# On-chip tiles declared in another order in a two-block attention decode kernel: the ring buffers start at byte 20480 of a partition instead of 16512

## The chip, the cores and the metric

The kernel runs on one core of a Trainium2 chip. The core has five engines that run side by side, each with its own instruction stream: TensorE (PE in the profile, with PEld for the loads of its weights), VectorE (DVE), ScalarE (ACT), GpSimd (POOL) and SyncE (SP). Data lies in the chip's main memory (DRAM in the program's names), in an on-chip tile memory of 128 partitions, and in a smaller accumulator memory that matmuls write. Sixteen DMA engines move data between main memory and the tile memory; SP and ACT issue transfers to them through queues of their own (q1 and q10 in the profile). Engines wait for each other and for transfers through semaphores.

The metric is the device time of one execution in microseconds. Before the change it is 1944.66 us, the median of 3 runs (1944.61 to 1944.73).

## What is computed

Two independent attention blocks, A and B, of the same shape: 2 batch rows, one query position, 32 heads of 192 elements, and a key and a value cache of 8192 positions for each head, all in bf16. The results stand side by side in the output of 2 x 1 x 1280.

```python
q = (x @ wq).reshape(B, Sq, H, Dh).transpose(0, 2, 1, 3)
scores = jnp.einsum("bhqd,bhkd->bhqk", q, k_cache) * (Dh ** -0.5)
p = softmax(scores, axis=-1)
o = jnp.einsum("bhqk,bhkd->bhqd", p, v_cache)
return o.transpose(0, 2, 1, 3).reshape(B, Sq, H * Dh) @ wo
# reference: concatenate([block(A), block(B)], axis=-1)
```

Each element of the caches is read once and used once. The caches of a block are 2 x 2 x 32 x 8192 x 192 x 2 B, so together they are 805 MB of the 836.77 MB that the profile counts as read.

## The kernel before

**Pairs.** The work is cut into 64 pairs of heads (2 blocks x 2 batch rows x 16). The K cache of a pair is 6,291,456 contiguous bytes. `kv_src` lays them over the 128 partitions, 49,152 B for each, so that partitions 0 to 63 hold the first head and 64 to 127 the second, with 128 positions in each partition. The V cache of a pair is laid out the same way.

**Tiles and their addresses.** `sb` allocates a tile of the tile memory. Tiles stand one behind the other in the order in which they are declared, each with the same address in every partition, and the first one of the kernel stands at byte 16512. In the order of the declarations these are three ring buffers (`ring`, 49,152 B in each partition), two product tiles (`prod`, 12,288 B), the q row (`qrow`, 12,288 B), then `qt`, `sc`, `pb` and a long list of small tiles, of which `filler` (1024 B) is one of the last. The two tiles of the result, `out_sb`, come almost at the end.

**Loads.** SP issues every large load, in the order of `order`: the q weights of both blocks first (each in two parts, one into a ring buffer, one into a product tile), then K and V of pair 0, K and V of pair 1, and so on; the last four are K, K, V, V. `next_slot` hands out the three ring buffers in turn. Before it reuses a buffer, SP waits until its last reader is done (`free`): the fourth multiply of a pair for K, the last matmul of the weighted sum for V. Behind the caches come the output weights `wo` in eleven pieces (`WA`, `WB`), which go into ring buffers as these come free; they are 160 to 3040 KB. The two loads of x and half of the stores of the result go through ACT's queue.

**One pair.** `add_q` copies the q of a pair into all partitions by a matmul, and `add_qt` takes it to the tile memory (`qt`). In four quarters VectorE multiplies K by q into `prod` (`add_mul`, line 290), TensorE sums over the 192 elements with twelve matmuls against the identity (`add_sum`, line 295), and VectorE reduces the 16 sums that are left into `sc` (`add_red`, line 301). Maximum (VectorE, GpSimd), exponential (ScalarE, into `pb`, line 322) and 64 matmuls of V with `pb` (line 334) follow. `add_fill` puts twelve matmuls on `filler` between them, whose results nobody reads. `add_place` collects the results of the heads, and at the end `add_contract` multiplies them by `wo`, ScalarE takes the sums to `out_sb`, and four small stores write the output.

**Loop.** VectorE, ScalarE and TensorE run pairs 2 to 61 in a hardware loop of three pairs a pass (`LOOP`), so a buffer with number i % 3 has a fixed address within a pass. SP's stream is written out.

The parts of the code that the change and the prediction speak of:

```python
ring = [sb(f"ring{i}", [128, RW], BF16) for i in range(3)]
prod = [sb(f"prod{i}", [128, TQ * Dh], BF16) for i in range(2)]
qrow = sb("qrow", [34, N], BF16)
...
load((kind, i), s, ring[s][:], src, free[s])
...
S_dve.add(lambda eng, t: eng.tensor_tensor(pr3(qd), quarter(i, qd), q, ALU.mult), waits=w, sig=("m", i, qd))
```

Of the kernel before, what the change touches and what calls it, by code (L numbers as in the profile page):

```python
# [8 lines left out]
BF16 = mybir.dt.bfloat16  # L9
F32 = mybir.dt.float32  # L10
# [91 lines left out]
def build_kernel(nc, blocks, out):  # L102
    NBLK = len(blocks)
    B, Hn, Sk, Dh = blocks[0]["k"].shape
# [6 lines left out]
    T = 128  # L111
    NB = 3
# [22 lines left out]
    with ExitStack() as es:  # L135
        sb = lambda name, shape, dt: es.enter_context(nc.sbuf_tensor(name, shape, dt))
        ps = lambda name, shape, dt: es.enter_context(nc.psum_tensor(name, shape, dt))
        sem = lambda name: es.enter_context(nc.semaphore(name))

        ring = [sb(f"ring{i}", [128, RW], BF16) for i in range(3)]  # L140
        prod = [sb(f"prod{i}", [128, TQ * Dh], BF16) for i in range(2)]
        qrow = sb("qrow", [34, N], BF16)
        qt = [sb(f"qt{i}", [128, Dh], BF16) for i in range(3)]
        sc = [sb(f"sc{i}", [128, T], F32) for i in range(NB)]
        pb = [sb(f"pb{i}", [128, T // 2, 34], BF16) for i in range(NB)]
        mp = [sb(f"mp{i}", [128, 2], F32) for i in range(NB)]
        mg = [sb(f"mg{i}", [128, 2], F32) for i in range(NB)]
# [8 lines left out]
        sel = sb("sel", [34, NBLK * B, 128], BF16)  # L156
        place = sb("place", [2, 264], BF16)
        ones = sb("ones", [128, 1], F32)
        filler = sb("filler", [128, 512], BF16)
        oallS = [sb(f"oallS{k}", [128, WR, 2], BF16) for k in range(NBLK)]  # L160
        out_sb = [sb(f"out_sb{k}", [34, NH2], BF16) for k in range(NBLK)]
        actd = sb("actd", [128, 2], F32)
# [360 lines left out]
def bass_concat_heads__gqa_block_cached__mha_block_cached__decode_kernel(  # L523
    nc: bass.Bass,
    A_x: bass.AP,
    A_k_cache: bass.AP,
    A_v_cache: bass.AP,
    A_wq: bass.AP,
    A_wo: bass.AP,
    B_x: bass.AP,  # L530
    B_k_cache: bass.AP,
    B_v_cache: bass.AP,
    B_wq: bass.AP,
    B_wo: bass.AP,
    out: bass.AP,
):
    blocks = [
        dict(x=A_x, k=A_k_cache, v=A_v_cache, wq=A_wq, wo=A_wo),
        dict(x=B_x, k=B_k_cache, v=B_v_cache, wq=B_wq, wo=B_wo),
    ]  # L540
    build_kernel(nc, blocks, out)
# [28 lines left out]
```

## Time and profile before

| What | Value |
|---|---|
| Median of 3 runs | 1944.66 us (1944.61 to 1944.73) |
| Execution that was profiled | 1944.61 us |
| Its span, first to last instruction | 1942.8 us |
| Mean granted TensorE clock | 0.996 |
| Read from main memory | 836.77 MB, 431 GB/s over the span |
| ACT busy | 187.0 us (10%) |
| POOL busy | 35.1 us (2%) |

The profile is one execution, recorded by the hardware. Its span leaves out what lies before the first and behind the last instruction of the program, 1.8 us here. Rows of the groups of instructions give line, engine, operation, what is written and read, and the count, then the total busy time and the mean time of one, then the idle time of the engine just before them and what ended most of it. A row of the waits names who waited for whom, with the total, the number of times and the longest. A DMA row gives the packets, the megabytes and the time that the packets took, as a share of the time of all 16 DMA engines in the stretch; a packet belongs to the stretch in which it starts. In the list of transfers the last number is the median time from issue to landing. The chain of waits is followed back from the last instruction to what released each step; its rows here are start, length and what it was, and "issue" is time in which the engine waited for nothing that the profile shows.

### The profile page before, as it was taken

To read this page: it belongs to the slowest core of one execution; us is meant where nothing else is said; L and a number is where in the kernel's file an instruction comes from. 1 tells how busy PE (TensorE), PEld (TensorE's weight loads), DVE (VectorE), ACT (ScalarE), POOL (GpSimd) and SP (SyncE) were. 2 spreads that over 40 slices of the span, in tenths; PEclk is the share of its full clock that TensorE was granted. 3 is DMA by queue.
4 is the path that set the end of the run, shared out by engine and by line. 5 is a ranking of instruction groups with operands and counts; after the bars stand their busy time and mean duration, and the time that the engine had idled before them with its cause. 6 is when DMAs were issued, how large, how long until landed. Compare 5 with 4: busy or idle time off the path is not lost.

```text
span 1942.8 us, 21605 instructions
## 1 busy us (share of the span) xinstructions
PE 1643.4 (85%) x8715; PEld 787.7 (41%) x8715; DVE 1081.4 (56%) x834; ACT 187.0 (10%) x608; POOL 35.1 (2%) x88
## 2 busy tenths in 40 slices
PE   4888888888888888888888888888888888888888
PEld 1343443443443443443443443443443443443434
DVE  0556546556646646656646646655645645655660
ACT  2111011011011011011011001001001001001000
POOL 1000000000000000000000000000000000000000
PEclk9999999999999999999999999999999999999999
DMA  9999999999999999999999999999999999999998
GB/s 414 430 431 434 434 431 432 435 434 430 432 436 433 428 435 434 432 430 436 434 429 432 437 433 429 433 436 434 429 433 434 434 430 434 433 433 431 435 427 377
DMA packets 20774, 836.98 MB, mean 431 GB/s; under 512 B 2316, under 2 KB 2584, under 8 KB 2968
## 3 DMA queue, kind: packets, MB, share of 16 engines
q1 hardware_dynamic: 20744, 836.78, 99.8%
q8 instruction: 10, 0.16, 0.0%
q14 instruction: 4, 0.03, 0.0%
q10 hardware_dynamic: 16, 0.01, 0.0%
HBM read 836.77 MB, written 0.01 MB: 431 GB/s over the span
## 4 chain that ended last, share of the span: by engine, by line
issue 87%; PE 4%; DMA 4%; DVE 3%; POOL 1%; ACT 0%; SPq 0%; POOLq 0%; DVEq 0%; ACTq 0%
DVE prod L290 2%; PE ops L334 2%; DMA ring<-in_B_wq_dram 2%; DMA ring<-in_B_k_cache_dram 1%; POOL mg L310 1%; PE scps L295 1%; DMA ring<-in_B_wo_dram 1%; PE ops L259 1%; DVE sc L301 0%; PE outps L342 0%; ACT pb L322 0%; PE outps L392 0%; SPq L189 0%; POOLq L49 0%; DVE mp L307 0%
## 5 line engine op out<-in xcount | busy, mean ns | idle before, releaser
L290 DVE TENSOR_TENSOR prod<-ring,qt 128x6144 bf16<-128x6144 bf16 x256 | 852.8, 3352 | 694.3 <-DMA ring<-in_B_k_cache_dram 324.3
L295 PE MATMUL scps<-prod,ident 128*128 128x512 bf16 x3072 | 709.1, 381 | 208.5 <-DVE prod L290 208.5
L334 PE MATMUL ops<-ring,pb 128*34 128x384 bf16 x4096 | 676.8, 326 | 0.0
L295 PEld LDWEIGHTS scps<-prod,ident 128*128 128x128 bf16 x3072 | 280.4, 98 | 614.6 <-DVE prod L290 309.0
L334 PEld LDWEIGHTS ops<-ring,pb 128*34 128x34 bf16 x4096 | 395.5, 98 | 258.7
L301 DVE TENSOR_REDUCE sc<-scps 128x32 f32<-128x512 f32 x256 | 175.6, 686 | 109.7 <-PE scps L295 109.7
L342 PE MATMUL outps<-filler,ident 128*128 128x512 bf16 x768 | 176.9, 380 | 0.0
L342 PEld LDWEIGHTS outps<-filler,ident 128*128 128x128 bf16 x768 | 70.1, 98 | 78.3
L357 ACT ACTIVATE oodd<-ops 2x192 f32<-2x192 f32 x64 | 20.6, 322 | 690.3 <-PE ops L334 690.3
L283 ACT ACTIVATE qt<-qps 64x192 bf16<-64x192 f32 x64 | 20.7, 324 | 662.5 <-PE qps L277 662.5
L322 ACT ACTIVATE pb<-sc,nb 64x128 bf16<-64x128 f32 x128 | 81.5, 637 | 7.8
L347 PE MATMUL ops<-ones,rs 128*2 128x1 f32 x128 | 12.2, 164 | 56.7 <-ACT pb L322 56.7
L310 POOL PARTITION_ALL_REDUCE mg<-mp x64 | 26.0, 406 | 1850.7 <-DVE mp L307 1850.7
L315 ACT ACTIVATE nb<-mg 64x1 f32<-64x1 f32 x64 | 13.0, 203 | 331.1 <-POOL mg L310 331.1
L347 PEld LDWEIGHTS ops<-ones,rs 128*2 128x2 f32 x128 | 5.5, 82 | 87.8 <-ACT pb L322 87.3
L322 ACT ACTIVATION_READ_ACCUMULATOR pb<-sc,nb 64x1 f32 x128 | 38.4, 300 | 0.0
L259 PE MATMUL ops<-ring,xT 128*2 128x512 bf16 x96 | 28.1, 420 | 6.2 <-issue 4.1
L277 PE MATMUL qps<-qrow,sel 34*128 (+1 forms) x64 | 21.3, 333 | 1.4 <-ACT qt L284 0.8
L377 PEld LDWEIGHTS oall<-on,place 2*128 (+1 forms) x256 | 10.3, 92 | 29.3 <-issue 26.3
L306 DVE TENSOR_REDUCE mp<-sc 64x1 f32<-64x128 f32 x64 | 17.8, 278 | 7.6
L361 DVE RECIPROCAL rc<-ops 2x1 f32<-2x1 f32 x64 | 9.4, 146 | 21.2 <-PE ops L334 21.2
L363 DVE TENSOR_TENSOR oodd<-ops,oodd 2x192 f32<-2x192 f32 x64 | 20.9, 326 | 0.4 <-ACT oodd L357 0.4
(43 smaller groups left out, 172.4 us busy)
## 6 DMA issues: line engine op xcount, KB each, us to landing
ring<-in_A_k_cache_dram SPq DMA_DIRECT2D x32, 6144.0 KB, 26.4
ring<-in_A_v_cache_dram SPq DMA_DIRECT2D x32, 6144.0 KB, 29.2
ring<-in_B_k_cache_dram SPq DMA_DIRECT2D x32, 6144.0 KB, 26.4
ring<-in_B_v_cache_dram SPq DMA_DIRECT2D x31, 6144.0 KB, 29.2
ring<-in_A_wq_dram SPq DMA_DIRECT2D x1, 6144.0 KB, 17.6
ring<-in_B_wq_dram SPq DMA_DIRECT2D x1, 6144.0 KB, 35.4
ring<-in_B_v_cache_dram SPq DMA_DIRECT2D x2, 3072.0 KB, 25.4
ring<-in_A_wo_dram SPq DMA_DIRECT2D x2, 3040.0 KB, 21.4
```

The lines of the kernel that those rows point to most:

```text
L259: ins = eng.matmul(ops[n % 2][32 * blk:32 * blk + 2, 0:QC], xT[:, c, 2 * blk:2 * blk + 2], src, start=(c == 0), stop=(c == DC - 1))
L277: return eng.matmul(qps[:, 0:2 * Dh], sel[:].rearrange("p s m -> p (s m)")[:, bass.ds(k, 128)], qrow[:, bass.ds(c, 2 * Dh)], start=True, s ...
L283: eng.activation(qt[i % 3][0:64, :], qps[0:64, 0:Dh], ACTF.Identity)
L290: S_dve.add(lambda eng, t: eng.tensor_tensor(pr3(qd), quarter(i, qd), q, ALU.mult), waits=w, sig=("m", i, qd))
L295: ins = eng.matmul(scps[qd % 2][:], ident[:], pr3(qd)[:, :, j * DG:(j + 1) * DG], start=(j == 0), stop=(j == NJ - 1))
L301: S_dve.add(lambda eng, t: eng.tensor_reduce(sc[i % NB][:, qd * TQ:(qd + 1) * TQ], scps[qd % 2][:], AXL.X, ALU.add), waits=[("s", i, qd), ...
L310: S_pool.add(lambda eng, t: eng.partition_all_reduce(mg[i % NB][:], mp[i % NB][:], 128, bass.bass_isa.ReduceOp.max), waits=[("mx", i), key ...
L322: ins = eng.activation(pb[i % NB][p0:p0 + 64, :, h::32], sc[i % NB][p0:p0 + 64, :].rearrange("p (j a) -> p j a", a=2), ACTF.Exp, bias=nb[i ...
L334: ins = eng.matmul(ops[i % NB][0:34, 0:2 * Dh], pb[i % NB][:, j, :], vv[:, j, :], start=(j == 0), stop=(j == T // 2 - 1))
L342: ins = eng.matmul(to, ident[:], filler[:], start=True, stop=True)
L357: S_act.add(lambda eng, t: eng.activation(oodd[i % NB][:], ops[i % NB][32:34, Dh:2 * Dh], ACTF.Identity), waits=[("pv", i), key("on", i - ...
L363: S_dve.add(lambda eng, t: eng.tensor_tensor(oodd[i % NB][:], ops[i % NB][0:2, 0:Dh], oodd[i % NB][:], ALU.add), waits=[("od", i)], sig=(" ...
```

## The change

The declarations of `qt`, `sc` and `filler` move in front of the ring buffers, and a tile `spare` of 256 B in each partition, which nothing reads or writes, is put between them. Everything else in the program is the same.

```diff
+        qt = [sb(f"qt{i}", [128, Dh], BF16) for i in range(3)]
+        sc = [sb(f"sc{i}", [128, T], F32) for i in range(NB)]
+        filler = sb("filler", [128, 512], BF16)
+        sb("spare", [128, 64], F32)
         ring = [sb(f"ring{i}", [128, RW], BF16) for i in range(3)]
         prod = [sb(f"prod{i}", [128, TQ * Dh], BF16) for i in range(2)]
         qrow = sb("qrow", [34, N], BF16)
-        qt = [sb(f"qt{i}", [128, Dh], BF16) for i in range(3)]
-        sc = [sb(f"sc{i}", [128, T], F32) for i in range(NB)]
         pb = [sb(f"pb{i}", [128, T // 2, 34], BF16) for i in range(NB)]
...
         ones = sb("ones", [128, 1], F32)
-        filler = sb("filler", [128, 512], BF16)
         oallS = [sb(f"oallS{k}", [128, WR, 2], BF16) for k in range(NBLK)]
```

## The prediction

> **What bounds the kernel now.** I read the page first: engine shares, DMA row, queue shares, transfer times.
>
> ```profile
> span 1942.8 us, 21605 instructions
> PE 1643.4 (85%) x8715; PEld 787.7 (41%) x8715; DVE 1081.4 (56%) x834; ACT 187.0 (10%) x608; POOL 35.1 (2%) x88
> ...
> DMA packets 20774, 836.98 MB, mean 431 GB/s; under 512 B 2316, under 2 KB 2584, under 8 KB 2968
> ...
> q1 hardware_dynamic: 20744, 836.78, 99.8%
> ...
> ring<-in_A_k_cache_dram SPq DMA_DIRECT2D x32, 6144.0 KB, 26.4
> ring<-in_A_v_cache_dram SPq DMA_DIRECT2D x32, 6144.0 KB, 29.2
> ```
>
> Queue q1, SP's loads, keeps the 16 DMA engines busy 99.8% of the span; no compute engine is above 85%. A K load lands 26.4 us after its issue and a V load 29.2 us. Then the waits of the engines, with those of SP's queue:
>
> ```profile
> DVE prod L290 <- DMA ring<-in_B_k_cache_dram: 324.3, 31, 10.7
> DVE prod L290 <- DMA ring<-in_A_k_cache_dram: 316.0, 31, 10.7
> ...
> SPq L189 <- PE ops L334: 1078.7, 64, 17.0
> SPq L189 <- DVE prod L290: 738.4, 64, 17.8
> ```
>
> VectorE waits for the K load of nearly every pair, about 10.3 us each time (640.3 / 62). SP waits as well, for ring buffers to come free, but that costs nothing as long as a transfer is queued ahead. To see this I took the chain of waits for the length of a pair of heads (one K and one V load) and a stretch of 1744.32 us from the middle:
>
> ```profile
> 162.66 28.64 issue
> ...
> 1790.70 28.47 issue
> ```
>
> ```profile
> DMA packets 17286, 754.98 MB, mean 433 GB/s; under 512 B 1920, under 2 KB 1920, under 8 KB 1920
> ...
> q1 hardware_dynamic: 17278, 754.88, 100.2%
> ```
>
> The two chain rows are 56 pairs apart: 1628.04 / 56 = 29.07 us a pair, 14.54 us a load. So a K load has 26.4 - 14.5 = 11.9 us of other transfers ahead of it when issued, a V load 14.7 us. The engines never lack work (100.2% of the stretch, which is over 100 because packets overlap a little). The kernel runs at the pace of its DMA engines, and only what changes their time per byte or per packet moves its end by much.
>
> **What a packet is.** In the stretch 1920 packets are under 512 B: 16 completion words for each of 120 loads. The other 15,358 carry 754.88 MB, 49,152 B each: one packet is one whole row of a ring buffer in one partition. Its start address is the tile's own.
>
> **The change, part by part.** No instruction, wait, transfer or order of issue is added, removed or moved; `spare` has no instruction. What moves is addresses. By the declared sizes, qt takes 3 x 384 B, sc 3 x 512 B, filler 1024 B, spare 256 B: 3968 B, and 16512 + 3968 = 20480, so the change does what it says. Each ring buffer is 49152 B = 12 x 4096, each product tile 12288 B = 3 x 4096: before, every one starts 128 B past a multiple of 4096, after, on one. The tiles from pb to ones move by 1280 B, those behind the filler by 256 B; qt and sc move in front. Their readers and writers are the compute engines, and two small loads and four small stores that lie at the ends.
>
> First, compute. What would it cost if the multiply, the sum matmuls or any small instruction ran differently at the new addresses? Nothing up to the cover: VectorE has about 10.3 us of waiting in each 29.07 us pair, TensorE 15% of the span, 4.4 us a pair. The groups that touch the moved tiles:
>
> ```profile
> L290 DVE TENSOR_TENSOR prod<-ring,qt 128x6144 bf16<-128x6144 bf16 x256 | 852.8, 3352 | 694.3 <-DMA ring<-in_B_k_cache_dram 324.3
> L295 PE MATMUL scps<-prod,ident 128*128 128x512 bf16 x3072 | 709.1, 381 | 208.5 <-DVE prod L290 208.5
> L334 PE MATMUL ops<-ring,pb 128*34 128x384 bf16 x4096 | 676.8, 326 | 0.0
> ```
>
> All four multiplies of a pair could become 20% slower (4 x 0.67 = 2.7 us) and the transfers would still be ahead. Without that cover, each 1% of the multiplies would cost 0.134 us a pair, 8.6 us in all. I cost compute at 0, both ways.
>
> Second, the transfers: time per byte and time per packet. The end of the kernel has many loads with short rows, so two stretches separate the two. From 1930 to 1936 us:
>
> ```profile
> DMA packets 430, 2.48 MB, mean 413 GB/s; under 512 B 50, under 2 KB 78, under 8 KB 383
> ...
> q1 hardware_dynamic: 426, 2.48, 99.9%
> ```
>
> Long rows: 100.2% of 1744.32 us x 16 engines, less 1920 words of 9 ns (below), over 15,358 rows = 1819.7 ns for 49,152 B. Short rows: 99.9% of 6 us x 16, less 50 words, over 376 rows = 253.9 ns for 6,596 B on average. The difference, 1565.8 ns for 42,556 B, is 36.79 ps per byte (435 GB/s over 16 engines). What is left, 253.9 - 242.7 = 11 ns, comes with each packet whatever its length; the rounding of the megabytes makes that uncertain by about 0.5 ns. So no part of the present address grows visibly with length: a penalty on every piece of a row is excluded up to the pace of 435 GB/s, and what the change can win lies in those 11 ns. In the stream a row takes 1744.32 / (15,358 / 16) = 1817.2 ns; less 1808.4 for its bytes and 1.1 for an eighth of a word, 7.7 ns. The rest overlaps.
>
> What of it hangs on the address? The rows that differ in little else are the four stores of the result, 640 B each, read from out_sb. With each tile's address rounded up to 32 B, out_sb0 lies at 225,120 and out_sb1 at 225,760, which is 96 and 224 B past a multiple of 256. The first block's two from ScalarE's queue, in 0.1 us; the second block's two from the same queue, then two from SP's, in 0.04 us each; and, in 0.1 us, ScalarE's last two with one completion word:
>
> ```profile
> q10 hardware_dynamic: 2, 0.00, 4.1%
> ```
>
> ```profile
> q10 hardware_dynamic: 2, 0.00, 10.9%
> ```
>
> ```profile
> q1 hardware_dynamic: 2, 0.00, 11.6%
> ```
>
> ```profile
> q10 hardware_dynamic: 3, 0.00, 4.9%
> ```
>
> Shares are of 16 engines: 4.1% x 1600 ns / 2 = 32.8 ns a packet for the first block; 10.9% x 640 / 2 = 34.9 and 11.6% x 640 / 2 = 37.1, mean 36.0, for the second. The same bytes from another phase took 3.2 ns longer. This is a read of the tile memory, where the ring loads write, and few packets. The last row says something else: 78.4 - 69.8 = 9 ns for a completion word, so a packet costs about 9 ns even with next to no data, which speaks for a fixed cost that no address removes.
>
> So a row's gain lies between 0 (all is packet handling) and 7.7 ns (all is the phase); a loss is bounded by the same 7.7 ns, since nothing in the trace shows an address on a multiple of 4096. I take 4.7 ns, a third of the way from the stores' 3.2 to the 7.7, because the stores alone isolate the address. There are 20,744 - 2,316 = 18,428 rows, 1,152 for each engine: 1,152 x 4.7 ns = 5.4 us; the ends are 0 and 8.9 us.
>
> [...]
>
> Third, the ends. Head and tail keep their length: the last piece of wo still lands after everything else, and the last products and the store follow it. The sum: span 1942.8 - 5.4 = 1937.4 us. Around the span lie 1944.61 - 1942.8 = 1.8 us of the profiled execution, which is within 0.05 us of the median of the runs, 1944.66. So 1939.2 us.
>
> **The rivals.** *The cost is the packet's, not the address's.* For it: the completion word's 9 ns with 4 B, near the 11 ns of a row. Against: the stores' 3.2 ns. Time 1944.6 us; a gain under 3.4 ns a row (3.9 us) falls here too.
>
> *All of the 7.7 ns goes.* For it: the long and short rows show one constant and no other term, and all rows share one phase. Against: the word's 9 ns. 1944.6 - 8.9 = 1935.7 us.
>
> *Slower: transfers and engines meet.* On multiples of 4096 the front of each row that is loaded, of the ring buffer that VectorE reads and of the product tile that TensorE reads all share low address bits zero, and if the tile memory serves them in blocks of such addresses, a write waits once a row for an engine's read. With the size that the phase has above, 4.7 ns, each row takes 1821.9 ns: 1944.6 + 5.4 = 1950.0 us. It decides from 3.4 ns a row on. Against: the ring buffers already lie at equal offsets from each other before, with VectorE and TensorE at work, and the stream is within 0.5% of its pace per byte. [...]
>
> **How the numbers follow.** About 0.2% (3.9 us) is what a measurement of this kernel can tell from no change. Forecast, 1937 to 1940.7 us around 1939.2: 0.53. All of the cost gone, 1934.5 to 1937: 0.09. No visible effect, 1940.8 to 1945: 0.24. Slower, 1948.5 to 1951.5: 0.14. Faster: 0.53 + 0.09 = 0.62; same 0.24; slower 0.14. The range runs from 1936.0 to 1945.2 us; it leaves out the slower case and half of the largest gain, 0.19.
>
> **What would show it.** Right: a pair takes 29.00 us instead of 29.07 in the chain, the middle stretch moves at 434 GB/s, the two-stretch sum leaves 6 to 7 ns a packet instead of 11, and the multiply and the matmuls keep 3352, 381 and 326 ns with VectorE still waiting for K loads. Wrong: the same 29.07 us and 11 ns (the packet's own cost), or a pair above 29.07 us with q1 still at 100% (transfers slowed), or VectorE no longer waiting for K loads (compute slowed beyond its cover).

## The result, and the profile after

The changed kernel takes 1939.87 us, the median of 11 runs (1939.65 to 1940.10), against 1944.61 us before (11 runs, 1944.36 to 1944.86). The ratio is 0.9976 with a 95% interval of 0.9966 to 0.9985: 4.74 us faster. The profiled execution after has a span of 1937.8 us, 5.0 us less. From its page, the engines, the DMA row and the queue:

```profile
span 1937.8 us, 21540 instructions
...
PE 1633.1 (84%) x8650; PEld 787.8 (41%) x8715; DVE 1081.4 (56%) x834; ACT 186.8 (10%) x608; POOL 34.9 (2%) x88
...
DMA packets 20774, 836.98 MB, mean 432 GB/s; under 512 B 2316, under 2 KB 2584, under 8 KB 2968
...
q1 hardware_dynamic: 20744, 836.78, 99.8%
```

Packets, bytes and the share of the load queue are what they were; the same work passes in less time. (The records of 64 matmuls on the filler and of one more matmul are missing from this trace, hence fewer instructions.) The groups that touch the moved tiles, with the wait of the multiply for its K loads:

```profile
L291 DVE TENSOR_TENSOR prod<-ring,qt 128x6144 bf16<-128x6144 bf16 x256 | 852.5, 3351 | 688.9 <-DMA ring<-in_B_k_cache_dram 322.1
L296 PE MATMUL scps<-prod,ident 128*128 128x512 bf16 x3072 | 709.0, 381 | 204.4 <-DVE prod L291 204.4
L335 PE MATMUL ops<-ring,pb 128*34 128x384 bf16 x4096 | 676.8, 326 | 0.0
```

These three kept their durations (3352, 381 and 326 ns before), and VectorE still waits for nearly every K load. The chain of waits, first and last row of the same 56 pairs:

```profile
162.88 28.52 issue
...
1786.88 28.41 issue
```

(1786.88 - 162.88) / 56 = 29.00 us a pair, where it was 29.07. The 56 pairs take 4.04 us less (1628.04 - 1624.00), which for 64 pairs is 4.6 us: the gain is spread over the whole stream of loads and lies in no single place. The DMA rows of the stretch of long rows (100 to 1839.36 us), then of the short rows near the end (1925 to 1931 us):

```profile
DMA packets 17281, 754.79 MB, mean 434 GB/s; under 512 B 1919, under 2 KB 1919, under 8 KB 1919
...
q1 hardware_dynamic: 17273, 754.69, 100.2%
```

```profile
DMA packets 384, 2.54 MB, mean 423 GB/s; under 512 B 43, under 2 KB 45, under 8 KB 311
...
q1 hardware_dynamic: 380, 2.54, 100.7%
```

By the working of the prediction: (100.2% x 1739.36 us x 16 - 1919 x 9 ns) / 15,354 = 1815.0 ns for a long row, 4.7 ns less than before; (100.7% x 6 us x 16 - 43 x 9 ns) / 337 = 285.7 ns for 7,537 B. That is 36.75 ps per byte, as before, and 8.7 ns for each packet, where it was 11.

### The profile page after: what moved, and what is told of

It is laid out like the page before. It is cut to its first block, busy times and chain, and to the rows that moved or that the text cites. A ratio compares the mean times of both kernels' runs of the same rounds, so it can differ in the third digit from the quotient of the medians.

```text
span 1937.8 us, 21540 instructions
## 1 busy us (share of the span) xinstructions
PE 1633.1 (84%) x8650; PEld 787.8 (41%) x8715; DVE 1081.4 (56%) x834; ACT 186.8 (10%) x608; POOL 34.9 (2%) x88
## 3 DMA queue, kind: packets, MB, share of 16 engines
q1 hardware_dynamic: 20744, 836.78, 99.8%
## 4 chain that ended last, share of the span: by engine, by line
issue 87%; PE 4%; DMA 4%; DVE 3%; POOL 1%; ACT 0%; SPq 0%; POOLq 0%; DVEq 0%; ACTq 0%
DVE prod L291 2%; PE ops L335 2%; DMA ring<-in_B_wq_dram 2%; DMA ring<-in_B_k_cache_dram 1%; POOL mg L311 1%; PE scps L296 1%; DMA ring<-in_B_wo_dram 1%; PE ops L260 1%; DVE sc L302 0%; PE outps L343 0%; ACT pb L323 0%; PE outps L393 0%; SPq L190 0%; POOLq L49 0%; DVE mp L308 0%
## 5 line engine op out<-in xcount | busy, mean ns | idle before, releaser
L291 DVE TENSOR_TENSOR prod<-ring,qt 128x6144 bf16<-128x6144 bf16 x256 | 852.5, 3351 | 688.9 <-DMA ring<-in_B_k_cache_dram 322.1
L343 PE MATMUL outps<-filler,ident 128*128 128x512 bf16 x704 | 162.4, 379 | 10.0 <-issue 9.9
```

The costliest lines, as they stand in the source:

```text
L343: ins = eng.matmul(to, ident[:], filler[:], start=True, stop=True)
```

## The experiments

### Which address matters

Four kernels follow, beside 31 runs of the kernel before with a median of 1944.62 us. The first takes the spare tile out of the changed kernel.

```diff
-        sb("spare", [128, 64], F32)
```

> The changed kernel without the spare tile: the ring buffers start at 20224 = 79 x 256, no multiple of 512 or 4096. Theory A (a row that starts 128 B past a multiple of 256 costs some 4 ns, and any multiple of 256 cures it): 1939.9 us. Theory B (the multiple of 4096 matters): 1944.6 us. Theory C (it is the place of qt, sc and filler in front of the ring buffers): 1939.9 us. Theory D (the product tiles' address matters to the engines, not the ring's to the transfers): 1939.9 us, as they move along.

1939.88 us, ratio 0.9975 (0.9966 to 0.9985). B is out: a multiple of 256 does as well as one of 4096. The second leaves the old order and puts 128 B in front.

```diff
+        sb("spare", [128, 32], F32)
         ring = [sb(f"ring{i}", [128, RW], BF16) for i in range(3)]
```

> The kernel before with nothing but a spare tile of 128 B in front of the ring buffers: they start at 16640 = 65 x 256, with qt, sc and filler where they stood, 128 B further. A and D: 1939.9 us. B and C: 1944.6 us.

1939.90 us, ratio 0.9975 (0.9966 to 0.9985). C is out, and one spare tile of 128 B does the whole work of the change. The third keeps the new order and goes off the boundary again.

```diff
-        sb("spare", [128, 64], F32)
+        sb("spare", [128, 96], F32)
```

> The changed kernel with a spare tile of 384 B instead of 256: the new order stays, but the ring buffers start at 20608, again 128 B past a multiple of 256. A, B and D: 1944.6 us. C: 1939.9 us.

1944.44 us, ratio 1.0000 (0.9991 to 1.0009): the gain is gone. The fourth separates the product tiles from the ring.

```diff
+        sb("spare2", [128, 32], F32)
         prod = [sb(f"prod{i}", [128, TQ * Dh], BF16) for i in range(2)]
```

> The changed kernel with 128 B between the ring buffers and the product tiles: the ring stays at 20480, the product tiles and the q row start 128 B past a multiple of 256. A, B and C: 1939.9 us, with all packets of a row still at one duration. D: 1944.6 us.

1939.93 us, ratio 0.9976 (0.9967 to 0.9985). D is out. What counts is the address of the ring buffers, where the loads write, and there only whether a row starts on a multiple of 256 B (16640, 20224 and 20480 do; 16512 and 20608 do not). The source of each row of a ring buffer starts on a multiple of 256 B from the start of its tensor in all these kernels. Whether the boundary counts by itself, or only against the phase of the source, was not tried.

### How far off, and which engine

Four kernels beside 33 runs of before with a median of 1944.24 us. The first two change the spare tile to 320 and 288 B.

```diff
-        sb("spare", [128, 64], F32)
+        sb("spare", [128, 80], F32)
```

> The changed kernel with 320 B spare: the ring buffers start at 20544, 64 B past a multiple of 256. A1 (any start off a multiple of 256 makes one piece more of each row, whatever the distance): 1944.6 us. A2 (cost in proportion to the distance, 4.1 ns a row at 128 B): half of it, 1942.2 us. A3 (a multiple of 64 is enough, 128 is a special case): 1939.9 us.

1944.18 us, ratio 1.0000 (0.9991 to 1.0009).

```diff
-        sb("spare", [128, 64], F32)
+        sb("spare", [128, 72], F32)
```

> The changed kernel with 288 B spare: the ring buffers start at 20512, 32 B past a multiple of 256. A1: 1944.6 us. A2: a quarter, 1941.1 us. A3 (64 is enough): 1944.6 us or more.

1945.45 us, ratio 1.0006 (0.9997 to 1.0015); its lowest run, 1945.18, is above the highest of the runs of before beside it, 1945.05. The traces agree: by their packets a long row takes 1820.8 ns on average from 100 us on with 32 B, and 1819.6 ns in the kernel before. A1's times hold to about 1 us: 64 B off costs what 128 B cost, and 32 B off does not cost a quarter but slightly more than 128. The one piece more of each row that A1 names is a supposition that no run shows. A2 and A3 are out.

The prediction priced the row as if its address cost by itself. Does it take an engine that uses the tile memory at the same time? Two cuts to the kernel before leave out most of what an engine does there. The first multiplies 16 of the 192 elements of each position:

```diff
-        q = qt[i % 3][:].unsqueeze(1).broadcast_to([128, TQ, Dh])
+        q = qt[i % 3][:].unsqueeze(1).broadcast_to([128, TQ, Dh])[:, :, 0:DG]
...
-        eng.tensor_tensor(pr3(qd), quarter(i, qd), q, ALU.mult)
+        eng.tensor_tensor(pr3(qd)[:, :, 0:DG], quarter(i, qd)[:, :, 0:DG], q, ALU.mult)
```

> The kernel before (ring at 16512) with the multiplies cut to 16 of the 192 elements of each position; the scores are sums over what the product tiles held. Theory E1 (the row's extra time comes only while VectorE reads the ring and writes the products): 1939.9 us, long rows at 1815 ns. E2 (while TensorE reads): 1944.6 us. E3 (the address costs by itself, no engine needed): 1944.6 us.

1944.55 us, ratio 1.0001 (0.9991 to 1.0011), with VectorE busy for 347.4 us instead of 1081.4. The second leaves out most of the matmuls:

```diff
-                for j in range(NJ):
+                for j in range(1):
...
-                for j in range(j0, j1):
+                for j in sorted({j0, j1 - 1}):
...
-        def add_fill(i, n=12, to=outps[:], waits=()):
+        def add_fill(i, n=1, to=outps[:], waits=()):
```

> The kernel before (ring at 16512) with one sum matmul a quarter instead of 12, two matmuls of V a pair instead of 64, and one filler matmul instead of 12; the output is then no attention. E1: 1944.6 us. E2: 1939.9 us, long rows at 1815 ns. E3: 1944.6 us. If both engines take part: between 1940 and 1944.6 us here and in the run with the light multiplies.

1943.63 us, ratio 0.9996 (0.9986 to 1.0006). One rival was left, that either engine alone is enough, so both cuts went into one kernel:

> The kernel before (ring at 16512) with both cuts at once: multiplies on 16 of 192 elements, one sum matmul a quarter, two matmuls of V a pair, one filler matmul; the output is then no attention. E3 (the address costs by itself, no engine needed): 1944.4 us, long rows as before. E4 (either engine alone is enough to disturb the transfers): 1939.9 us, long rows at 1815 ns.

1943.98 us beside 1944.27 us of before (26 runs), ratio 0.9998 (0.9988 to 1.0008). In its groups, the multiply and the two groups of matmuls:

```profile
L290 DVE TENSOR_TENSOR prod<-ring,qt 128x512 bf16<-128x512 bf16 x256 | 102.0, 419 | 1514.7 <-DMA ring<-in_A_k_cache_dram 779.3
L295 PE MATMUL scps<-prod,ident 128*128 128x512 bf16 x256 | 143.4, 611 | 938.4 <-DVE prod L290 938.4
L334 PE MATMUL ops<-ring,pb 128*34 128x384 bf16 x130 | 53.5, 515 | 411.8 <-DMA ring<-in_B_v_cache_dram 209.8
```

These three took 2238.7 us together before and take 298.9 us here, and the time hardly moves. Nor do the rows. The DMA row from 100 to 1800 us:

```profile
DMA packets 16850, 736.01 MB, mean 433 GB/s; under 512 B 1872, under 2 KB 1872, under 8 KB 1872
...
q1 hardware_dynamic: 16845, 735.96, 100.2%
```

(100.2% x 1700 us x 16 - 1872 x 9 ns) / 14,973 = 1819 ns for a long row, as before the change. E1, E2 and E4 are out; E3 holds. What slows the rows is not the work of VectorE and TensorE.

### By the row or by the byte, and does each row pay?

Two kernels split each K and V load but the last into two halves, so that there are twice as many rows of half the length, once off the boundary and once on it. The edit is the same in the kernel before and in the changed one:

```diff
-                load((kind, i), s, ring[s][:], src, free[s])
+                load((kind, i), s, ring[s][:, 0:RW // 2], src[:, 0:RW // 2], free[s])
+                load((kind, i), s, ring[s][:, RW // 2:RW], src[:, RW // 2:RW], [])
```

> The kernel before (ring at 16512) with each K and V load but the last split into two of 24,576 B rows: twice the rows, the same bytes. Theory P (the address costs by the row): 9.2 to 9.4 us above the same split at 20480. Theory Q (it costs by the byte or by time in the stream): 4.7 us above it. Both count some 5 us more than unsplit for the fixed part of a row and about 1 us for the added completion words: P 1954 to 1956 us, Q 1950 us.

> The changed kernel (ring at 20480) with the same split loads. Both theories: 1939.9 us plus 1,024 rows more for each engine at 4 to 8 ns each, and about 1 us of completion words: 1945 to 1949 us.

1953.95 us off the boundary, ratio 1.0050 (1.0036 to 1.0063), and 1945.17 us on it, ratio 1.0004 (0.9995 to 1.0013). The difference is 8.78 us, where whole rows gave 4.74. Each engine has 127 x 8 = 1,016 rows more, so 2,168 instead of 1,152: 8.78 us / 2,168 = 4.05 ns a row, 4.74 / 1,152 = 4.11 ns. P holds, a little under the 9.2 to 9.4 us that it forecast, and Q with its 4.7 us is out: it is a cost by the row. The DMA rows of the two from 100 to 1800 us, off the boundary and then on it:

```profile
DMA packets 33511, 732.09 MB, mean 431 GB/s; under 512 B 3718, under 2 KB 3718, under 8 KB 3718
...
q1 hardware_dynamic: 33502, 731.99, 100.4%
```

```profile
DMA packets 33656, 735.26 MB, mean 433 GB/s; under 512 B 3734, under 2 KB 3734, under 8 KB 3734
...
q1 hardware_dynamic: 33647, 735.16, 100.4%
```

At the same share, 29,913 rows pass on the boundary and 29,784 off it: less the words at 9 ns, 911.8 against 915.8 ns a row.

Then one buffer of the three alone, in the changed kernel:

```diff
-        ring = [sb(f"ring{i}", [128, RW], BF16) for i in range(3)]
+        ring = [sb("ring0", [128, RW], BF16)]
+        sb("spare1", [128, 32], F32)
+        ring.append(sb("ring1", [128, RW], BF16))
+        sb("spare2", [128, 32], F32)
+        ring.append(sb("ring2", [128, RW], BF16))
```

> The changed kernel with 128 B in front of the second ring buffer and 128 B behind it: only this buffer, which takes every third load, starts 128 B past a multiple of 256. Theory R (each row off the boundary pays its own 4 ns): a third of 4.7 us, 1941.4 us. Theory S (the rows on the boundary leave slack that takes it up): 1939.9 us.

1939.64 us, ratio 0.9976 (0.9966 to 0.9985): 4.63 us under the 1944.27 us of the kernel before, as with all three buffers on the boundary. R fails, and the time is the one that S gives. A third of the rows off the boundary costs nothing that shows. Its DMA rows from 100 to 1800 us:

```profile
DMA packets 16883, 737.53 MB, mean 434 GB/s; under 512 B 1872, under 2 KB 1872, under 8 KB 1872
...
q1 hardware_dynamic: 16875, 737.43, 100.2%
```

It is the pace of the changed kernel, 434 GB/s, for the rows of all three buffers. The packets of the trace say more than S: 16,414 of the 16,512 long rows took 1815 ns, as 16,417 did in the changed kernel. So the rows off the boundary are not late with the others making up for it; they pass at full pace themselves. In the kernel before only 3,218 rows took 1815 ns, and most of the others 1816 to 1824. Two buffers off the boundary were not tried.

The trace of before bears on this as well. If rows off the boundary can pass without cost for a while, the first loads should run as fast off the boundary as on it. Three short stretches that hold no completion word, so that share divided by packets is the time of a row: the kernel before from 42 to 45 us, the same from 74 to 80 us, and the changed kernel from 60 to 66 us.

```profile
DMA packets 27, 1.33 MB, mean 442 GB/s; under 512 B 0, under 2 KB 0, under 8 KB 0
...
q1 hardware_dynamic: 27, 1.33, 102.1%
```

```profile
DMA packets 51, 2.51 MB, mean 418 GB/s; under 512 B 0, under 2 KB 0, under 8 KB 0
...
q1 hardware_dynamic: 51, 2.51, 96.7%
```

```profile
DMA packets 52, 2.56 MB, mean 426 GB/s; under 512 B 0, under 2 KB 0, under 8 KB 0
...
q1 hardware_dynamic: 52, 2.56, 98.3%
```

102.1% x 3 us x 16 / 27 = 1815 ns: 40 us into the span, a row off the boundary takes what a row on it takes. 30 us later it is 96.7% x 6 us x 16 / 51 = 1820 ns. The changed kernel has 98.3% x 6 us x 16 / 52 = 1815 ns. The last digit of a share is worth 1 to 2 ns here. The pace does not stay at 1820 ns from there on, as the kernel before from 118 to 124 us shows:

```profile
DMA packets 53, 2.61 MB, mean 434 GB/s; under 512 B 0, under 2 KB 0, under 8 KB 0
...
q1 hardware_dynamic: 53, 2.61, 100.3%
```

100.3% x 6 us x 16 / 53 = 1817 ns. By the packets of the trace, 124 of the 128 long rows that start from 39 us on took 1815 ns, 49 to 78 in each of the five groups of 128 that start from 68 to 126 us, and 23 in the group from 199 us on. So the cost comes in by degrees over some 160 us, and in the whole middle stretch a row takes 1819.7 ns on average.

## Why the prediction was right, and where its reasons were not

**The bound** was read rightly. The load queue is at 99.8% before and after, a pair takes the 29.00 us that was forecast, and neither a multiply of a twelfth of its elements nor the loss of most of TensorE's matmuls moves the end by more than 0.7 us.

**Compute at 0** holds: 3351, 381 and 326 ns after, and the product tiles' address does not show in the time (1939.93 us with them 128 B past a multiple of 256).

**The price of a row** was 4.7 ns by the prediction and is 4.1 ns (4.74 us over 1,152 rows), and that makes the difference between the 5.4 us of the sum and the 4.74 us measured. The cost is by the row, as the two stretches had it, and nearly doubles when the rows nearly double (8.78 us for 2,168 rows). That holds for the long rows. Among the pieces of `wo`, by the packets of the traces, rows of 7680 B took 294.4 ns on average before and 291.0 after, and of the 260 rows of 1280 B in the kernel 232 took 55 ns before and 251 after: there, next to nothing was left to win.

**What the price was made from** is the weak step. "The stores alone isolate the address" was not so. The second block's stores do take as long after the change, when out_sb has kept its distance from a multiple of 256. Its two from SP's queue, with one completion word, from 1936.76 to 1936.82 us:

```profile
q1 hardware_dynamic: 3, 0.00, 8.3%
```

(8.3% x 960 ns - 9 ns) / 2 = 35 ns a packet. But the kernel with only 128 B in front swaps the two distances: out_sb0 is then 224 B past a multiple of 256 and out_sb1 96 B. ScalarE's two stores of the first block there, from 1927.7 to 1927.9 us, and its two of the second block with one word, from 1937.18 to 1937.22 us:

```profile
q10 hardware_dynamic: 2, 0.00, 2.0%
```

```profile
q10 hardware_dynamic: 3, 0.00, 11.1%
```

The first block's stay at 2.0% x 3200 ns / 2 = 32 ns, and the second block's fall to (11.1% x 640 ns - 9 ns) / 2 = 31 ns. So the distance is worth some 4 ns in the second block, and nothing that shows in the first, whose stores run among the loads of `wo`. The 3.2 ns came out of comparing the one with the other. They are also reads of 640 B at the end, and the loads follow another rule. For the loads, the distance does not set the size (32 B costs no less than 128 B), a third of the rows off the boundary costs nothing, and with 128 B the rows around 40 us cost nothing. The prediction had each row pay for itself, and forecast that the constant of a packet would fall from 11 to 6 or 7 ns; it fell to 8.7. That a third of the way between 3.2 and 7.7 ns landed near 4.1 is luck: neither end measures what the address costs a load.

**The rivals.** That the cost is the packet's own is right for what is left: on the boundary, 1,016 rows more still cost 5.5 us (1945.17 against the 1939.64 us of the unsplit loads with one buffer off), completion words included. That all 7.7 ns go is wrong: 4.74 us went and not 8.9, and the records keep 8.7 ns with each packet. That engines and transfers meet on multiples of 4096 is out, since nothing became slower, and 20224 and 20480 give the same time to 0.01 us.

**What stays open** is why a third of the rows is free, and why the cost comes in by degrees. A row passes in 1815 ns whether all rows or two thirds of them are on the boundary, so something other than its address sets that pace. What it is was not shown, nor why 124 of 128 rows pass in 1815 ns at 39 us and 23 of 128 at 199 us.

## What to carry to other kernels

Where the loads bound a kernel, as here at 99.8% of the span, try the tiles that they write on a multiple of 256 B; a spare tile of 128 B was all it took here, for 0.24% (1939.90 against 1944.62 us). The price went with the number of rows and not with the bytes: at half the length, 24,576 B, the same fault cost 8.8 us instead of 4.7. Rows of 1280 B had next to nothing to gain here (of 260, 232 took 55 ns before and 251 after), and one buffer of three off the boundary cost nothing (1939.64 us, against 1939.87 with all three on it). And a cost per packet that is read from a trace should be looked for at the start of the stream too, before it is priced as if each packet paid it.

## What was not expected of the hardware

Rows that start 128 B off the boundary run at full pace 40 us into the span (1815 ns) and come to their 1820 ns on average only by degrees, at 200 us or so. The average is the same with most of the work of VectorE and TensorE left out (1819 ns). One ring buffer of three off the boundary costs nothing (1939.64 us, and its rows too take 1815 ns). A start 32 B off costs at least what 128 B cost (1945.45 against 1944.24 us). The stores of the result show their distance from the boundary at the very end (35 ns a packet at 224 B, 31 at 96) and not among the loads (32 ns at 224 B, 33 at 96).
